# Tail-token loads split by head instead of by batch, and tail-token stores in one transfer, in a fused retention + SoLU kernel

## The chip, the cores and the metric

The kernel runs on one core of a Trainium2 chip. The metric is the device time of one execution in microseconds; the median of three runs is compared. A profile of one execution stands beside it. In the profile PE is the matmul engine (TensorE), PEld its weight loads, DVE the vector engine, ACT the scalar engine, POOL GpSimd, and SP the engine that issues nearly all transfers ("SPq" is its queue). The transfers themselves are carried out by 16 DMA engines.

## The reference

Eight batches, eight heads, 576 tokens per batch, head size 64. First a decayed causal attention without softmax, then a feed-forward layer with a SoLU and a layer norm on all 4608 tokens:

```python
scores = scale * q @ k.T                         # (8, 8, 576, 576)
ret    = scores * gamma_h ** (i - j) for j <= i  # else 0
x      = (ret @ v).transpose(0, 2, 1, 3).reshape(4608, 512)
h      = x @ w_in                                # (4608, 1024)
solu   = h * softmax(h)
ln     = (solu - mean) / sqrt(var + 1e-6) * g_ln
out    = ln @ w_out                              # (4608, 512), float32
```

## The kernel before

The 576 tokens of a batch are cut into two windows of 256 tokens and a rest of 64, the "tail". The tails of four batches together make one more window of 256 tokens, so that a group of four batches has nine windows and both groups have 18 (`WINS`; a window with index 2 is a tail). Each window is worked on in two halves of four heads: 36 steps `i`. The steps of the tails are 16 and 17 (batches 0 to 3) and 34 and 35 (batches 4 to 7). On the output side a window gives two tiles of 128 tokens: 36 tiles `t`, of which 16, 17, 34 and 35 hold tail tokens, two batches of 64 each.

For each step the kernel loads q, k and v (`load`: `ldq16` is the q of step 16) into buffers `rawq`, `rawk`, `rawv`, five of each, and scales or casts them to 16 bits (`sq`, `sk` at L394, `cv` at L399, in the main part of the kernel all on POOL). A full step is one transfer of 256 KB for each of q, k and v. A tail step is four transfers of 64 KB for each. TensorE transposes (L419, L429), forms scores (`S`, L508), the inter-window part and the product with v (L472); DVE applies the mask; ACT moves the result to `xT` (L576). For each tile TensorE then computes `M1` (L587), ACT the exponential (L595), DVE the SoLU and its statistics, TensorE transposes and computes `M2` (L660), and ACT scales and evicts it to `o_sb` (`oe`, L669). There are three buffers `o_sb`. `store` (`out16` is the store of tile 16) sends 128 rows of 2 KB to DRAM: whole tiles at L680, tail tiles at L685 in two transfers of 64 rows.

The order on every engine is fixed. `plan()` lists all operations with what they depend on and which buffers they hold, `FIRST` and `LAST` write out the order by hand for the start and the end, and in between each operation has a due time; `order_ops` turns that into the start order, and `emit` issues it. `parts` tells the planner how many transfers an operation has. SP issues in this order too: an issue that waits for a buffer or for a completion holds up all that stand behind it. Of the last tile only the second half of the eviction (`oz`) and the store are issued after a branch on a value that the kernel computes (`tc.If`); the other side of that branch, a slower general path, is not executed with these inputs.

The instructions that move the tail tokens in the built program have these shapes (outermost first, in elements): a tail load reads 32x4x128 from DRAM and writes 32x4x128; a tail store reads 64x512 and writes 64x512.

Of the kernel before, what the change touches and what calls it, by code (L numbers as in the profile page):

```python
# [308 lines left out]
def kernel(  # L309
# [10 lines left out]
    nc = tc.nc  # L320
    _, H, S, D = q.shape
# [46 lines left out]
    tk = [dict() for _ in range(NT)]  # L368
# [4 lines left out]
    def load(i, nm, src):  # L373
        w, hf = divmod(i, 2)
        b, wi = WINS[w]
        hh = slice(4 * hf, 4 * hf + 4)
        st[i]["r" + nm] = t = pools["raw"].tile([P, 4, 2, D], FP, tag=nm, name="raw" + nm)
        if wi < 2:
            nc.sync.dma_start(
                out=t, in_=src[b, hh, 256 * wi : 256 * wi + 256, :].rearrange("h (p j) d -> p h j d", j=2)  # L380
            )
        else:
            for r in range(4):
                nc.sync.dma_start(
                    out=t[32 * r : 32 * r + 32],
                    in_=src[b + r, hh, 512:S, :].rearrange("h (p j) d -> p h j d", j=2),
                )

    def scale(i, nm, base, eng):
# [283 lines left out]
    def store(t):  # L673
        w, c = divmod(t, 2)
        b, wi = WINS[w]
        if wi < 2:
            r0 = b * S + 256 * wi + P * c
            n = 64 if 22 <= t < 28 else P
            for r in range(0, P, n):
                nc.sync.dma_start(out=out[r0 + r : r0 + r + n, :], in_=tk[t]["osb"][r : r + n])  # L680
        else:
            for r in range(2):
                r0 = (b + 2 * c + r) * S + 512
                q_dma = nc.scalar if t == NT - 1 and r else nc.sync
                q_dma.dma_start(out=out[r0 : r0 + 64, :], in_=tk[t]["osb"][64 * r : 64 * r + 64])  # L685

    w_in_v = moe_w_in.rearrange("(c p) f -> p c f", p=P)
    w2_v = moe_w_out.rearrange("(c p) m -> p c m", p=P)
# [60 lines left out]
    def emit(o):  # L749
# [4 lines left out]
        tt = {"DVE": nc.vector, "POOL": nc.gpsimd}.get(eng)  # L754
        if k_ in ("ldq", "ldk", "ldv"):
            load(x, k_[2], dict(q=q, k=k, v=v)[k_[2]])
        elif k_ == "sq":
            scale(x, "q", 0, tt)
# [6 lines left out]
        elif k_ == "Le":  # L765
            tk[x]["lo"] = lo = 8 if wide(f"L{x}") else 8 * (x % 2)
            tk[x]["ev"] = tl_ev("first" if wide(f"L{x}") else "last", lo, lo + 8)
        elif k_ == "TL":
            st[x + 2]["ev"] = tk[x - 4]["ev"] = tl_ev(x, 0, 16)
            tk[x - 4]["lo"] = 8  # L770
        elif k_ in ("bnA", "bnB"):
            stats(x, k_ == "bnB")
        elif k_ == "lwi":
            w_load(x, w_in_v)
        elif k_ == "lwo":
            w_load(x, w2_v)
        elif k_ == "wg":
            w2_cast(x, eng)
        elif k_ == "gc":
            nc.vector.tensor_copy(out=gln, in_=cur["g"][:, 0:8])  # L780
        elif k_ == "cnt":
            count_a()
        elif k_ == "cs":
            count_b()
        elif k_ == "ci":
            nc.vector.tensor_copy(out=count, in_=cur["cs"][0:1, 0:1])
        elif name[:2] == "wi":
            w_in_cast(int(name[2]), name[3] == "b", copy)
        else:
            dict(  # L790
                T=qk_tp, L=ln_tp, K=kv_mm, I=inter, st=state, sc=state_cast, sm=state_next, S=scores, mask=mask, V=av, xe=x_ev, M1_=mm1,
                ex=exp_, so=solu, va=squares, fx=sums2, fin=final, rs=rstd, M2_=mm2, oe=o_ev, out=store, wc=w2_center,
                M=lambda _: mm2(NT - 1, 1), oz=lambda _: o_ev(NT - 1, 1), G=lambda _: g_tp(), WM=lambda _: w2_sum(), wm=lambda _: w2_mean(),
            )[k_](x)
# [4 lines left out]
    with tc.manual_schedule():  # L799
# [6 lines left out]
        for x in sbd[0]:  # L806
# [3 lines left out]
            out=ident, in_=ident, pattern=[[1, P]], compare_op=ALU.is_equal, fill=0.0, base=0, channel_multiplier=-1  # L810
        )
        tri = masks.rearrange("p m (j jq q) -> p m j jq q", j=2, jq=2)
        for n, first in ((P, P), (64, 0)):
            nc.gpsimd.affine_select(
                out=tri[:n, 0], in_=tri[:n, 0], pattern=[[-1, 2], [1, 2], [2, 64]], compare_op=ALU.is_ge,
# [100 lines left out]
    with tc.If(in_range < NT * P, preferred_fallthrough_block=False) as cmp:  # L916
        with tc.For_i(0, NT, 1) as t:
            general(t)
        for b in range(B):
            r0 = (b // 4 * 18 + b % 4 * 4) * P  # L920
            nc.sync.dma_start(out=out[b * S : b * S + 512, :], in_=rows[r0 : r0 + 512, :])
        for b in range(0, B, 4):
            r0 = (b // 4 * 18 + 16) * P
            nc.sync.dma_start(
                out=out[b * S : (b + 4) * S, :].rearrange("(b s) m -> b s m", s=S)[:, 512:S],
                in_=rows[r0 : r0 + 256, :].rearrange("(b s) m -> b s m", b=4),
            )
    with cmp.Else():
        o_ev(NT - 1, 1)
        store(NT - 1)  # L930
# [30 lines left out]
```

## Time and profile before

| | |
|---|---|
| Runs | 212.8, 212.13, 214.13 us; median 212.8 |
| Span of the profiled execution, first to last instruction | 210.9 us (the runs lie 1.2 to 3.2 us above it; its own whole time is not listed apart) |
| PE busy | 200.8 us, 95% of the span |
| DVE, ACT, POOL busy | 79%, 67%, 67% |
| Granted TensorE clock | 0.999 |
| Transfers | 64814 packets, 42.66 MB, 202 GB/s on average |

A row of the page's part on transfers gives the tile, the queue, the number of issues, the KB of each and the median time from issue to landing. A row of a timeline gives the start, the length, the engine, the line, the operation with its tiles and shapes, the number of instructions merged into the row, and in brackets the idle time before it and what ended it. For SPq the length is that of the issue, not of the transfer. A table of stages gives the busy time of each engine in a stretch of the span; its last two columns are the share of the 16 DMA engines' time that packets took and the GB/s moved.

### The profile page before, as it was taken

What the parts mean: (1) busy time and instruction counts of PE and PEld (TensorE: products, weight loads), DVE (VectorE), ACT (ScalarE), POOL (GpSimd) and SP (SyncE); (2) the same over time, 40 slices, a digit from 0 to 9 for tenths busy, and PEclk for the clock granted to TensorE, in tenths of its full rate; (3) what the DMA queues carried; (4) which work ended last, traced back from release to release, by engine and by line L of the source; (5) the groups of instructions that cost most, each with busy time, mean ns of one, the idle gap of its engine ahead of it and who ended that gap; (6) DMA issues with size and microseconds to landing.
All of it is one profiled execution on the core that took longest, in us unless ns stands there. A gap on an engine that the chain in (4) does not pass through costs nothing. (4 is left out here: it accounts for less than half of the span.)

```text
span 210.9 us, 10171 instructions
## 1 busy us (share of the span) xinstructions
PE 200.8 (95%) x4400; PEld 113.2 (54%) x4400; DVE 166.1 (79%) x279; ACT 141.7 (67%) x235; POOL 141.7 (67%) x240
## 2 busy tenths in 40 slices
PE   7986989999999999999999999999999999999992
PEld 2442654665566555555555555555666555554451
DVE  6565779997868898978898898889988998753760
ACT  2375787897666776776666777666767777573752
POOL 7434758999997975948787979797979792001110
PEclk9999999999999999999999999999999999999999
DMA  5999999999666559778999686776355222311224
GB/s 157 345 355 334 329 311 269 301 293 306 195 188 188 169 139 278 217 214 259 314 288 305 198 252 183 217 234 181 94 152 153 54 57 67 71 63 54 101 101 104
DMA packets 64814, 42.66 MB, mean 202 GB/s; under 512 B 3320, under 2 KB 58624, under 8 KB 64768
## 3 DMA queue, kind: packets, MB, share of 16 engines
q1 hardware_dynamic: 64528, 41.82, 68.4%
q8 instruction: 34, 0.56, 1.2%
q10 hardware_dynamic: 240, 0.18, 0.5%
q14 instruction: 12, 0.10, 0.2%
HBM read 32.55 MB, written 9.44 MB: 199 GB/s over the span
## 5 line engine op out<-in xcount | busy, mean ns | idle before, releaser
L587 PE MATMUL h_ps<-w_in,xT 128*128 128x512 f16 x288 | 68.5, 380 | 0.0
L660 PE MATMUL o_ps<-w2c,ev 128*128 128x512 f16 (+1 forms) x296 | 67.6, 373 | 0.0
L610 DVE TENSOR_TENSOR solu<-h_ps,e_sb 128x1024 f16<-128x1024 f32 x32 | 39.2, 1223 | 16.7 <-ACT e_sb L595 16.5
L595 ACT ACTIVATE e_sb<-h_ps 128x1024 f32<-128x1024 f32 x36 | 36.8, 1023 | 21.9 <-PE h_ps L587 20.4
L540 DVE TENSOR_TENSOR ret<-s_ps,masks 128x1024 f16<-128x1024 f32 x36 | 43.9, 1220 | 6.0 <-PE s_ps L508 5.4
L660 PEld LDWEIGHTS <-ev 128*128 128x128 f16 x296 | 28.7, 98 | 32.7
L616 DVE BATCH_NORM_STATS2 bs<-solu 128x6 f32<-128x512 f16 x64 | 43.6, 685 | 0.9
L587 PEld LDWEIGHTS <-xT 128*128 128x128 f16 x288 | 25.3, 98 | 29.1 <-ACT xT L576 0.8
L394 POOL TENSOR_TENSOR q<-rawq,small 128x512 f16<-128x512 f32 x34 | 35.4, 1042 | 7.3 <-DMA rawq<-in_q_dram 5.9
L669 ACT ACTIVATE o_sb<-o_ps,rs 128x512 f32<-128x512 f32 (+1 forms) x37 | 25.0, 676 | 21.8 <-PE o_ps L660 10.4
L394 POOL TENSOR_TENSOR k<-rawk,small 128x512 f16<-128x512 f32 x34 | 35.4, 1042 | 6.0 <-DMA rawk<-in_k_dram 5.9
L457 ACT COPY ev<-tl 128x1024 f32<-128x1024 f32 (+1 forms) x32 | 29.7, 932 | 4.7 <-PE tl L429 4.2
L576 ACT CAST xT<-xy 128x512 f16<-128x512 f32 x36 | 26.7, 742 | 3.0 <-PE xy L472 2.9
L571 POOL CAST sbd<-gg 64x256 f16<-64x256 f32 x64 | 25.4, 397 | 3.0
L562 POOL TENSOR_TENSOR gg<-gt,small 128x128 f32<-128x128 f32 x32 | 13.1, 409 | 16.9 <-DVE gt L557 16.5
L648 POOL TENSOR_TENSOR w<-mv,w 128x2 f32<-128x2 f32 x16 | 3.1, 194 | 27.8 <-ACT w L633 13.9
L399 POOL CAST v<-rawv 128x512 f16<-128x512 f32 x28 | 17.1, 609 | 0.2
L508 PE MATMUL s_ps<-ev 64*64 64x128 f16 x576 | 14.8, 218 | 0.3
L472 PE MATMUL xy<-ret,v 64*64 64x128 f16 x576 | 14.7, 217 | 0.0
L472 PEld LDWEIGHTS <-sbd 128*128 128x128 f16 x128 | 9.3, 98 | 9.3 <-issue 1.1
L446 PE MATMUL tl<-ident,solu 64*64 64x64 f16 x1024 | 14.2, 195 | 0.0
L846 PE MATMUL tl<-zeros 128*128 128x512 f16 x41 | 12.7, 445 | 1.3 <-DVE zeros L802 1.3
(71 smaller groups left out, 214.6 us busy)
## 6 DMA issues: line engine op xcount, KB each, us to landing
rawq<-in_q_dram SPq DMA_DIRECT2D x32, 256.0 KB, 5.1
rawk<-in_k_dram SPq DMA_DIRECT2D x32, 256.0 KB, 5.3
rawv<-in_v_dram SPq DMA_DIRECT2D x32, 256.0 KB, 5.1
out_dram<-o_sb SPq DMA_DIRECT2D x26, 256.0 KB, 3.1
out_dram<-o_sb SPq DMA_DIRECT2D x19, 128.0 KB, 2.3
wst<-in_moe_w_in_dram SPq DMA_DIRECT2D x4, 512.0 KB, 6.8
wst<-in_moe_w_out_dram SPq DMA_DIRECT2D x4, 512.0 KB, 7.1
rawq<-in_q_dram SPq DMA_DIRECT2D x16, 64.0 KB, 2.4
```

What stands on the lines that cost most here:

```text
L394: eng.tensor_tensor(out=t.rearrange("p j h d -> p h j d"), in0=st[i]["r" + nm], in1=g, op=ALU.mult)
L457: nc.scalar.copy(out=t[:, lo:hi].rearrange("p x (r w) -> p r x w", r=2), in_=tls[n].rearrange("p r x w -> p (r x w)").bitcast(FP).rearrang ...
L472: nc.tensor.matmul(start=(c, e) not in begun, stop=False, skip_group_check=True, **kw)
L540: nc.vector.tensor_tensor(out=d["ret"].rearrange("p e h j q -> p (e h) (j q)"), in0=d["s"].rearrange("p e h j q -> p (e h) (j q)"), in1=ma ...
L571: nc.gpsimd.tensor_copy(out=t[ee[e], :, :, ee[e]], in_=st[i]["gg"][ee[e]])
L576: nc.scalar.copy(out=xT[:, 2 * w : 2 * w + 2, 2 * hf : 2 * hf + 2].rearrange("p c h (q j) -> p c h j q", j=2), in_=xys[i][:, :, 0:256].rea ...
L587: nc.tensor.matmul(out=h_ps[:, hh], lhsT=xT[:, t, dc], rhs=w_in16[:, dc, hh], start=(dc == 0), stop=(dc == 3),)
L595: nc.scalar.activation(out=d["e"], in_=d["h"], func=ACT.Exp, accum_out=se[:, t : t + 1])
L610: nc.vector.tensor_tensor(out=d["solu"], in0=d["h"], in1=d["e"], op=ALU.mult)
L616: nc.vector.bn_stats(out=d["bs"][:, half], in_=d["solu"][:, half * 512 : half * 512 + 512])
L660: nc.tensor.matmul(out=o, lhsT=d["ev"][:, d["lo"] + c], rhs=w2c16[:, c, mm], start=(c == 0), stop=(c == 7))
L669: nc.scalar.activation(out=d["osb"][:, mm], in_=d["o", half], func=ACT.Copy, scale=ws[t // 2]["rs"][:, t % 2 : t % 2 + 1])
```

## The change

In `load`, a tail step still issues four transfers of 64 KB for each of q, k and v. Each was one batch with four heads on 32 partitions; each is now one head with four batches on 128 partitions. In `store`, a tail tile other than the last goes in one transfer of 128 rows and no longer in two of 64. The last tile keeps its two halves on two queues. The planner is not touched, so the order of all operations on all engines stays; SP issues three transfers fewer (tiles 16, 17 and 34).

```diff
         else:
-            for r in range(4):
+            for h in range(4):
                 nc.sync.dma_start(
-                    out=t[32 * r : 32 * r + 32],
-                    in_=src[b + r, hh, 512:S, :].rearrange("h (p j) d -> p h j d", j=2),
+                    out=t[:, h].rearrange("p j d -> p (j d)"),
+                    in_=src[b : b + 4, 4 * hf + h, 512:S, :].rearrange("r (p j) d -> r p (j d)", j=2),
                 )
...
         else:
-            for r in range(2):
-                r0 = (b + 2 * c + r) * S + 512
-                q_dma = nc.scalar if t == NT - 1 and r else nc.sync
-                q_dma.dma_start(out=out[r0 : r0 + 64, :], in_=tk[t]["osb"][64 * r : 64 * r + 64])
+            rows_t = out.rearrange("(b s) m -> b s m", s=S)[b + 2 * c : b + 2 * c + 2, 512:S]
+            if t < NT - 1:
+                nc.sync.dma_start(out=rows_t, in_=tk[t]["osb"])
+            else:
+                for r in range(2):
+                    (nc.scalar if r else nc.sync).dma_start(out=rows_t[r], in_=tk[t]["osb"][64 * r : 64 * r + 64])
```

In the built program a tail load now reads 4x32x128 from DRAM and writes 128x1x128 on the SBUF side; a tail store reads 128x512 and writes 2x64x512. The store stands at L684 in the changed file (L687 for the last tile).

## The prediction

> **What bounds the kernel now.** I read the page's part 1 first, then the table by stage, then the waits of SP's queue, then the transfers.
>
> ```profile
> PE 200.8 (95%) x4400; PEld 113.2 (54%) x4400; DVE 166.1 (79%) x279; ACT 141.7 (67%) x235; POOL 141.7 (67%) x240
> 20.00:48.00 28.00, 25.45 (x456) 15.63 (x459) 23.78 (x42) 23.23 (x42) 23.52 (x36) 1.00 1.12 303
> 160.00:205.00 45.00, 45.00 (x852) 23.96 (x851) 32.96 (x53) 28.91 (x50) 16.07 (x29) 1.00 0.28 80
> SPq L680 <- ACT o_sb L669: 53.8, 24, 5.3
> ```
>
> The second and third rows are stages: length, busy time of PE, PEld, DVE, ACT, POOL, granted clock, share of the 16 DMA engines, GB/s. TensorE is busy 95% of the span and 45.00 of 45.00 us late on: whatever stops it there is not won back. From 20 to 48 us the transfers are the limit (share above 1, 303 GB/s). SP waits 53.8 us for results to store, so its own issue time is covered in most places. TensorE needs the tail loads only through POOL; POOL's last wait for a transfer ends long before the first of them is used:
>
> ```profile
> 33.26 1.04 POOL L394 TENSOR_TENSOR k<-rawk,small 128x512 f16<-128x512 f32 x1 [0.22 <-DMA rawk<-in_k_dram]
> ```
>
> So a faster tail load earns nothing (POOL's waits from 36 us on name no transfer at all). The question is whether the new shapes make transfers slow enough to reach a buffer that ACT or POOL needs, or the end.
>
> **The change part by part.**
>
> *How many DMA engines carry a transfer.* Three windows of the DMA view each hold few transfers of one queue (packets, MB, share of 16 engines):
>
> ```profile
> q10 hardware_dynamic: 160, 0.04, 10.7%
> small<-small ACTq DMA_DIRECT2D x1, 39.0 KB, 2.4
> g_rows<-in_moe_g_ln_dram ACTq DMA_DIRECT2D x1, 4.0 KB
> ...
> q1 hardware_dynamic: 144, 0.26, 13.9%
> out_dram<-o_sb SPq DMA_DIRECT2D x1, 256.0 KB, 2.0
> ...
> q1 hardware_dynamic: 160, 0.26, 22.8%
> out_dram<-o_sb SPq DMA_DIRECT2D x2, 128.0 KB, 2.2
> ```
>
> The second (190 to 195 us) is one store of 128 rows: 144 packets, so 16 beside the data. The third (182 to 187) is two stores of 64 rows: 160 = 128 + 2x16. The first (0 to 4) is 128 rows of `small` and 8 rows of `g_rows`: 160 = 136 + 24, that is 16 + 8. One closing packet per engine in use explains all three: transfers with 128 or 64 outermost rows ran on 16 engines, the one with 8 on 8. The page's own sum agrees:
>
> ```profile
> q1 hardware_dynamic: 64528, 41.82, 68.4%
> rawq<-in_q_dram SPq DMA_DIRECT2D x16, 64.0 KB, 2.4
> rawk<-in_k_dram SPq DMA_DIRECT2D x16, 64.0 KB, 3.4
> ```
>
> Counting 512 packets for each of 96 whole loads, 128 for each of 48 tail loads (these are 64 KB, two of the three kinds shown), 128 and 256 for the two kinds of weights (4 each), 128 for 26 stores and 64 for 19, and 16 more for each of these 197 transfers, I get 64528. So the tail loads of 32 partitions also ran on 16 engines.
>
> The changed program's instructions carry, on the DRAM side, 4x32x128 for a tail load (outermost count 4: the batches) and 2x64x512 for a tail store (outermost 2), against 128 on the SBUF side; before, both sides began with 32 or 64. No transfer of this trace has different outermost counts on its two sides. Bounds: 16 engines as now (the SBUF side decides), or 4 and 2 (the smaller decides). The nearest row is `g_rows`, where an outermost count under 16 set the engines; I take 4 and 2.
>
> The Trainium skill, "DMA: Bandwidth & Descriptors", section "Why a DMA increments its semaphore by 16 and not by 1", says that the engine count is the largest number up to 16 that divides the slowest dimension on both sides. By that rule it is 4 and 2; the same page's advice under "Rules for kernel authors" to use one 128-partition transfer instead of two halves speaks for the change, and without the first rule the sum below would be zero.
>
> *Prices.* One store row of 2 KB: 13.9% of 16 engines in 5 us is 11.1 us over 128 rows, 87 ns. On two engines a store is 64 rows each, 5.6 us, against 0.7 us now. Fixed part: 2.0 us to landing less 0.7, so 1.3 us. Upper bound per row: the 64-row stores, 22.8% of 80 us over 128 rows, 142 ns. A whole 256 KB load at 303 GB/s takes 0.865 us, 16 KB on each engine; a 64 KB tail load on four engines also puts 16 KB on each, so it costs engines 0 to 3 as much as a whole load: 0.865 us, a tile 3.5 us.
>
> *Issues.* Loads stay 48 issues; stores lose three, of 0.55 us each (the L685 row below). The first two are covered by SP's waits for results; at the end the saved issue (from about 206.5, 0.55 long) lies before SP waits for the last half's result, which ACT ends at 206.75 + 0.47 = 207.22. Price 0; without the cover, -0.6.
>
> *The last stores.*
>
> ```profile
> 205.95 1.89 SPq L685 DMA_DIRECT2D out_dram<-o_sb  x3
> 206.75 0.47 ACT L669 ACTIVATE o_sb<-o_ps,rs 128x256 f32<-128x256 f32 x1 [0.41 <-PEq L916]
> 207.37 0.47 SPq L685 DMA_DIRECT2D out_dram<-o_sb  x1
> L685 SPq DMA_DIRECT2D out_dram<-o_sb x7: 466/551/757, 128.4 to 207.4; - x7
> DMA to landing us min/median/max: 2.3/2.5/2.9
> ```
>
> Tile 34's halves leave at 205.95 and about 206.5; the last half of tile 35 at 207.37 lands near 207.37 + 2.5 = 209.9, and the span ends 1.0 us later. After: tile 34 holds two engines for 5.6 us from 205.95, to 211.5; both halves of tile 35 leave four rows each on the same engines, 0.7 us; with 1.3 fixed, 213.5. That is +3.6 us (bounds: 0 on 16 engines; +7.1 at 142 ns).
>
> *The stores of tiles 16 and 17, then the loads of windows 34 and 35.* SP issues in a fixed order, and in the built program each transfer waits for the eighth before it.
>
> ```profile
> 128.39 1.19 SPq L685 DMA_DIRECT2D out_dram<-o_sb  x2
> 129.68 0.53 SPq L379 DMA_DIRECT2D rawq<-in_q_dram  x1
> ...
> 133.23 1.28 SPq L685 DMA_DIRECT2D out_dram<-o_sb  x2
> ...
> 138.28 0.36 SPq L680 DMA_DIRECT2D out_dram<-o_sb  x1
> ...
> 143.23 0.36 SPq L680 DMA_DIRECT2D out_dram<-o_sb  x1
> 143.68 2.48 SPq L384 DMA_DIRECT2D rawq<-in_q_dram  x4
> ...
> 151.42 1.15 SPq L680 DMA_DIRECT2D out_dram<-o_sb  x1
> ...
> 156.51 2.94 SPq L384 DMA_DIRECT2D rawv<-in_v_dram  x4
> 159.55 0.38 SPq L680 DMA_DIRECT2D out_dram<-o_sb  x1
> 162.29 0.69 ACT L669 ACTIVATE o_sb<-o_ps,rs 128x512 f32<-128x512 f32 x1 [0.61 <-PE o_ps L660]
> 167.23 0.69 ACT L669 ACTIVATE o_sb<-o_ps,rs 128x512 f32<-128x512 f32 x1 [0.66 <-POOL w L648]
> 168.06 0.41 PE L508 MATMUL s_ps<-ev 64*64 64x128 f16 x16
> ```
>
> Between two of these stores stand three whole loads (2.6 us per engine). On engine 0 from 128.4: store 5.6, loads 2.6, store 5.6, loads 2.6, store 0.7, loads 2.6, store 0.7: 20.4 us, so it is free at 148.8, where the tail loads already wait. Then 24 tail loads (20.8) and two stores (1.4) take it to 171.0. The store issued at 159.55 (tile 21) thus lands at 172.3. `o_sb` has three buffers, so the eviction of tile 24, at 167.23 now, waits 5.1 us. Behind it on ACT stand every later eviction and cast; on TensorE the next score product (168.06) needs the PSUM bank that this eviction reads until 167.92, so TensorE stops at once: 5.1 less 0.1, **+5.0 us**. The store at 151.42 (12 tail loads earlier) lands at 161.2, 1.1 us ahead of the eviction at 162.29. Bounds: 0 on 16 engines; at 142 ns two stores of 9.1 us add 7.0, so +12.
>
> *The first group, windows 16 and 17.*
>
> ```profile
> 53.27 2.62 SPq L384 DMA_DIRECT2D rawq<-in_q_dram  x4
> ...
> 75.89 1.83 SPq L384 DMA_DIRECT2D rawv<-in_v_dram  x4
> 86.08 0.61 POOL L399 CAST v<-rawv 128x512 f16<-128x512 f32 x1
> DMA to landing us min/median/max: 2.9/5.1/9.2
> ```
>
> From the first of these tiles to the last (four tiles between), engines 0 to 3 get six tiles 20.8 us, five whole loads 4.3, four stores 2.8: 27.9 from 53.3 is 81.2; with 2.9 - 0.9 = 2.0 for a load's landing (last row, L379) 83.2, while POOL casts it at 86.08. The cover is 2.9 us, price 0. If the engines stand idle in between, where SP waits for results, it goes: bound +4, as after that POOL's waits would be TensorE's.
>
> *Sum.* 0 + 3.6 + 5.0 + 0 = +8.6 us: the span goes from 210.9 to 219.5. The runs lie 1.2 to 3.2 above the span; on their median of 212.8 I forecast **221.4 us**.
>
> **The rivals.**
> *All transfers stay on 16 engines* (the SBUF side decides). For it: every 128-partition transfer here has 16. Against: `g_rows`. Then loads and landings stay, three issues go: 212.8, not slower. It decides where a 64 KB tail load still closes with 16 packets.
> *Only the end counts.* Engines 0 and 1 keep up: a row costs two engines alone less than 87 ns, or the backlog at 143.7 is worked off while SP waits. For it: only 1.1 and 5.1 us of lateness hang on sums of 20 us, and a tenth faster rows take most of it. Then +3.6: 216.4.
> *Two engines run at the 64-row price.* 142 ns a row: +7.1 and +12, 231.9. For it: that row, measured on 16 engines reading 64 partitions. Against: the new source is 128 partitions, as in the 87 ns row.
>
> **How the numbers follow.** Forecast, tail transfers on few engines with a stall at tile 24 and a late end: 0.62, own range 217.5 to 227 (the stall 1 to 6.5, the end 3.5 to 4, the first group 0 to 4). Only the end: 0.16. Sixteen engines: 0.12. The dear rows: 0.10. The range 215 to 228 leaves out the sixteen and the dear rows. About 1% (2.1 us) can be told from no change here: sixteen engines would be same, 0.10, or with luck at the end faster, 0.02; all else is slower, 0.88.
>
> **What would show it.** Queue q1 would hold 63862 packets: 64528 less 48x12 for loads closing with 4, less 3x30 for stores closing with 2; at 16 engines 64480. A store at L684 would land near 7 us, not 2.0 to 3.1. In the waits, ACT would wait once for a transfer of tile 21 near 167 us, and TensorE's busy share would drop there; the end would show SP idle some 3.6 us longer after its last issue. Wrong: tail loads landing in 2 to 3.5 us as now, or no gap on ACT near 167 us, or POOL waiting for `rawv` near 86 us, which would move the loss to the first group.

## The result and the profile after

The changed kernel takes 220.99 us (median of 6 runs, 220.62 to 222.46) against 212.77 us (6 runs): ratio 1.0394, 95% interval 1.0363 to 1.0426. Here and below the ratios compare runs in the chip's faster state alone and are not exactly the quotients of the medians given. The profiled execution has a span of 219.9 us, 9.0 us more than before.

From the page of the changed kernel, the busy times, the main queue (packets, MB, share of 16 engines) and the transfers:

```profile
PE 201.4 (92%) x4400; PEld 113.8 (52%) x4400; DVE 166.1 (76%) x279; ACT 141.5 (64%) x235; POOL 141.7 (64%) x240
q1 hardware_dynamic: 63862, 41.82, 64.5%
rawq<-in_q_dram SPq DMA_DIRECT2D x16, 64.0 KB
```

No engine has more instructions to work through than before: TensorE is busy 201.4 us against 200.8 for the same 4400 products and waits the rest. The packets are 63862, to the packet what loads closing on 4 engines and stores closing on 2 give. The rows of the transfers have no median time to landing at their end here, so the landings of the changed kernel are read from the waits and from the DMA view.

The two places of the loss stand in the waits of the engines and of SP's queue (total us, times, longest):

```profile
ACT o_sb L669 <- DMA out_dram<-o_sb: 2.7, 1, 2.7
PE s_ps L508 <- ACT o_sb L669: 1.7, 1, 1.7
SPq L918 <- SPq L918: 6.4, 1, 6.4
```

The first two are not in the profile before. The third stands there at L916, the same place in the file before:

```profile
SPq L916 <- SPq L916: 0.8, 2, 0.5
```

The first two, in order of time on ACT and TensorE of the changed kernel:

```profile
163.49 0.69 ACT L669 ACTIVATE o_sb<-o_ps,rs 128x512 f32<-128x512 f32 x1 [0.61 <-PE o_ps L660]
...
170.50 0.69 ACT L669 ACTIVATE o_sb<-o_ps,rs 128x512 f32<-128x512 f32 x1 [2.67 <-DMA out_dram<-o_sb]
...
171.24 0.42 PE L508 MATMUL s_ps<-ev 64*64 64x128 f16 x16 [1.73 <-ACT o_sb L669]
```

The eviction of tile 23 is 1.2 us later than before (162.29), that of tile 24 is 3.3 us later (167.23): some 2.0 us are lost between them, and TensorE stands still at the score product behind it. The rest is at the end (the issues of SP for tile 34 and for its half of tile 35):

```profile
209.14 0.64 SPq L684 DMA_DIRECT2D out_dram<-o_sb  x1
210.71 0.50 SPq L687 DMA_DIRECT2D out_dram<-o_sb  x1
```

SP's last issue is 3.3 us later than before (207.37), and from there to the end of the span it takes 9.2 us against 3.5: 5.7 us more. 1.2 + 2.0 + 5.7 is 8.9 of the 9.0 us.

How the four engines are kept busy shows in the DMA view of the changed kernel from 146 to 167 us, in 40 slices (busy tenths of 16 engines, then GB/s):

```profile
DMA  9999422222223222222268232224222222222422
GB/s 307 321 360 384 131 69 92 89 87 84 86 86 104 85 86 87 86 83 86 88 194 319 76 98 87 84 88 117 86 87 88 86 87 86 86 86 88 117 87 86
```

A level of 2 tenths and 86 GB/s: four of sixteen engines work without a break, the others rest except where a whole load, a store on 16 engines or another queue's packets pass. 64 KB at 86 GB/s is 0.76 us.

### The profile page after: what moved, and what is told of

Same layout as the page of the kernel before. It is cut to its first block, busy times and chain, and to the rows that moved or that the text cites. A ratio compares the mean times of both kernels' runs of the same rounds, so it can differ in the third digit from the quotient of the medians.

```text
span 219.9 us, 10167 instructions
## 1 busy us (share of the span) xinstructions
PE 201.4 (92%) x4400; PEld 113.8 (52%) x4400; DVE 166.1 (76%) x279; ACT 141.5 (64%) x235; POOL 141.7 (64%) x240
## 3 DMA queue, kind: packets, MB, share of 16 engines
q1 hardware_dynamic: 63862, 41.82, 64.5%
## 5 line engine op out<-in xcount | busy, mean ns | idle before, releaser
L540 DVE TENSOR_TENSOR ret<-s_ps,masks 128x1024 f16<-128x1024 f32 x36 | 43.9, 1220 | 10.1 <-PE s_ps L508 9.6
L446 PEld LDWEIGHTS <-solu 64*64 64x64 f16 x1024 | 10.9, 109 | 5.5 <-issue 2.9
```

Source lines behind the costliest of these rows:

```text
L446: nc.tensor.transpose(out=x[ee[e], r, c], in_=src[ee[r], P * c + 64 * e : P * c + 64 * e + 64], identity=ident[ee[r], ee[r]],)
L540: nc.vector.tensor_tensor(out=d["ret"].rearrange("p e h j q -> p (e h) (j q)"), in0=d["s"].rearrange("p e h j q -> p (e h) (j q)"), in1=ma ...
```

## The experiments

The runs are compared with the kernel before on the same chip; intervals are at 95%. The first four take the change apart.

**Loads only.**

The edit, against the kernel before; the stores stay as there:

```diff
-            for r in range(4):
+            for h in range(4):
                 nc.sync.dma_start(
-                    out=t[32 * r : 32 * r + 32],
-                    in_=src[b + r, hh, 512:S, :].rearrange("h (p j) d -> p h j d", j=2),
+                    out=t[:, h].rearrange("p j d -> p (j d)"),
+                    in_=src[b : b + 4, 4 * hf + h, 512:S, :].rearrange("r (p j) d -> r p (j d)", j=2),
                 )
```

> Tail loads by head, tail stores as before. Theory 'few engines': the loads run on four engines (queue q1 64528 - 576 = 63952 packets), a load costs these engines 0.76 us (86 GB/s over four engines in the late stretch of the changed kernel). Without the two slow stores of tiles 16 and 17 there is no backlog at 143.7 us, so 24 loads (18.2 us), two stores (1.4) and 1.3 fixed bring tile 21 to 164.6 us, before the eviction at 167.2: no stall, 212.8 to 214.0 us. Rival 'the loads alone make the stall': about 3.3 us slower than before, 216 us.

213.32 us against 213.46: ratio 1.0009 (0.9972 to 1.0047), 63952 packets. The loads do run on four engines, and alone they cost nothing that the times can show. ACT's eviction of tile 24 has its usual short wait for POOL:

```profile
167.54 0.69 ACT L669 ACTIVATE o_sb<-o_ps,rs 128x512 f32<-128x512 f32 x1 [0.66 <-POOL w L648]
```

**Stores only.**

The edit, against the changed kernel; the stores stay as there:

```diff
-            for h in range(4):
+            for r in range(4):
                 nc.sync.dma_start(
-                    out=t[:, h].rearrange("p j d -> p (j d)"),
-                    in_=src[b : b + 4, 4 * hf + h, 512:S, :].rearrange("r (p j) d -> r p (j d)", j=2),
+                    out=t[32 * r : 32 * r + 32],
+                    in_=src[b + r, hh, 512:S, :].rearrange("h (p j) d -> p h j d", j=2),
                 )
```

> Tail stores of tiles 16, 17 and 34 in one transfer, tail loads as before. Theory 'few engines': 64528 - 90 = 64438 packets; the stores of tiles 16 and 17 put some 5 us of backlog on two engines, which is hidden without the slow loads; the store of tile 34 costs 5.7 us at the end as in the changed kernel: 218.5 us, and no wait of ACT for a transfer. Rival 'the stall belongs to the stores': 221 us, with a wait of ACT near 167 us. Rival 'the end is a price of the loads too': under 217 us.

219.79 us, ratio 1.0303 (1.0213 to 1.0393), 64438 packets, no wait of an eviction on ACT for a store. The eviction of tile 24 has its short wait for POOL again:

```profile
168.52 0.69 ACT L669 ACTIVATE o_sb<-o_ps,rs 128x512 f32<-128x512 f32 x1 [0.66 <-POOL w L648]
```

The two slow stores in the middle are hidden: in this trace the evictions of tiles 16 to 19, behind which they run, take 14.8 us, as in the kernel before. The time is 1.3 us above the 218.5 expected, and as much above the next run, which has the last of the three stores alone. Of these 1.3 us, 0.8 stand in the two profiles ahead of the first tail transfer (the first eviction of an output tile starts at 47.9 us here and at 47.1 there), so they are not the price of a store.

**Only the store of tile 34.**

The edit, against the changed kernel (the queue is chosen so that tiles 16 and 17 stay on SP's):

```diff
-            if t < NT - 1:
+            if t == NT - 2:
...
-                    (nc.scalar if r else nc.sync).dma_start(out=rows_t[r], in_=tk[t]["osb"][64 * r : 64 * r + 64])
+                    (nc.scalar if r and t == NT - 1 else nc.sync).dma_start(out=rows_t[r], in_=tk[t]["osb"][64 * r : 64 * r + 64])
```

The loads go by batch, as in the kernel before.

> Only the store of tile 34 goes in one transfer; all else as before. Theory 'few engines': 64528 - 30 = 64498 packets, the same time as with all three stores, 218.5 us (+5.7), all of it behind SP's last issue. Rival 'the end is late because of what came earlier': 212.8 us.

218.48 us, ratio 1.0252 (1.0174 to 1.0331), 64498 packets. SP's queue of this kernel:

```profile
206.24 0.63 SPq L684 DMA_DIRECT2D out_dram<-o_sb  x1
207.53 0.51 SPq L687 DMA_DIRECT2D out_dram<-o_sb  x1
```

The waits of SP's queue in it:

```profile
SPq L918 <- SPq L918: 6.5, 1, 6.5
```

And the head of its page:

```profile
span 216.8 us, 10170 instructions
```

Up to the last issue it is level with the kernel before (207.53 against 207.37); then SP waits 6.5 us. Some 5 us of the loss (5.0 on the medians, 5.9 on the spans) belong to one instruction.

**The same shapes with tokens outermost.**

```diff
-  src[b : b + 4, 4 * hf + h, 512:S, :].rearrange("r (p j) d -> r p (j d)", j=2)
+  src[b : b + 4, 4 * hf + h, 512:S, :].rearrange("r (p j) d -> p r (j d)", j=2)
...
-  nc.sync.dma_start(out=rows_t, in_=tk[t]["osb"])
+  nc.sync.dma_start(out=rows_t.rearrange("r s m -> s r m"), in_=tk[t]["osb"])
```

> As the changed kernel (loads by head to 128 partitions, stores in one transfer of 128 rows), but the DRAM side names the same bytes with tokens outermost: 32x4x128 and 64x2x512 instead of 4x32x128 and 2x64x512. The tail tokens thus come to other partitions and other output rows than they should, so the tail part of the output is not the reference's; the work and the bytes are the same. Theory 'the outermost count sets the engines': 16 engines again, 64480 packets, 212.8 us within 0.7. Rival 'the shape is slow, not the count of engines' (128 partitions of 512 B, two blocks of DRAM in one store): 221 us as the changed kernel.

213.80 us against 213.46, ratio 1.0014 (0.9979 to 1.0050), and the queue's row of this kernel reads

```profile
q1 hardware_dynamic: 64480, 41.82, 66.8%
```

The same bytes, the same 128 partitions, the same number of issues, two blocks of DRAM in one store: all of the loss is gone with 16 closing packets back. It is the outermost count on the DRAM side, not the shape on the SBUF side. The order in which the bytes are walked changed with the count; that it is the count rests on the closing packets and on the 86 GB/s above. The run also shows what the change is worth without that fault: nothing. It is no replacement as it stands, since it puts the tail tokens on other partitions and other output rows; the rest of the kernel would have to follow.

The next four separate the two losses and test what stands between cause and time.

**Without the store of tile 34.**

```diff
-            if t < NT - 1:
+            if t < NT - 2:
...
-                    (nc.scalar if r else nc.sync).dma_start(out=rows_t[r], in_=tk[t]["osb"][64 * r : 64 * r + 64])
+                    (nc.scalar if r and t == NT - 1 else nc.sync).dma_start(out=rows_t[r], in_=tk[t]["osb"][64 * r : 64 * r + 64])
```

> The changed kernel, but tile 34 goes in two halves as before. Theory 'two separate losses': the end term of 5.7 us goes and the stall at tile 24 stays: 2.0 to 3.3 us over the kernel before, 215 to 216 us, with ACT waiting once for a transfer near 167 us. Rival 'all of it is the end': within 1 us of the kernel before.

215.72 us against 213.09, ratio 1.0096 (1.0061 to 1.0132). So about 1% is lost without the slow end, and the stall at tile 24 is there by itself:

```profile
169.82 0.69 ACT L669 ACTIVATE o_sb<-o_ps,rs 128x512 f32<-128x512 f32 x1 [2.11 <-DMA out_dram<-o_sb]
```

**Loads by head and the store of tile 34, tiles 16 and 17 in halves.**

```diff
-            if t < NT - 1:
+            if t == NT - 2:
...
-                    (nc.scalar if r else nc.sync).dma_start(out=rows_t[r], in_=tk[t]["osb"][64 * r : 64 * r + 64])
+                    (nc.scalar if r and t == NT - 1 else nc.sync).dma_start(out=rows_t[r], in_=tk[t]["osb"][64 * r : 64 * r + 64])
```

> The changed kernel, but tiles 16 and 17 go in two halves as before; loads by head and the one store of tile 34 stay. Theory 'the stall needs the backlog of both stores and the loads': no wait of ACT for a transfer, 5.7 us over the kernel before, 218.5 us. Rival 'the loads plus ordinary traffic suffice': the stall stays, 220.5 to 221 us.

218.68 us, ratio 1.0259 (1.0186 to 1.0332), no wait of an eviction on ACT for a store. So the stall needs both: the loads (absent in "stores only") and the two stores (absent here).

**Four buffers `o_sb`.**

```diff
-    e=2, solu=4, osb=3, tl=1, tlx=2, tlT=1, tlL=1, wst=5,
+    e=2, solu=4, osb=4, tl=1, tlx=2, tlT=1, tlL=1, wst=5,
```

> The changed kernel with four o_sb buffers instead of three; the order of all instructions is the same. Theory 'tile 24 waits for the buffer of tile 21': the eviction of tile 24 then needs tile 20, which lands earlier, so the stall of 2.0 us goes: 219 us. Rival 'the late transfers would stop something else instead' (POOL waiting for the loads of step 35): 221 us as the changed kernel.

219.77 us, ratio 1.0289 (1.0207 to 1.0371). No eviction waits for a store any more, and that of tile 24 has again the short wait for POOL:

```profile
169.06 0.69 ACT L669 ACTIVATE o_sb<-o_ps,rs 128x512 f32<-128x512 f32 x1 [0.66 <-POOL w L648]
```

The buffer was the link; no other wait took its place. The interval overlaps that of the changed kernel, so the trace carries this verdict, not the time.

**The store of tile 34 behind the branch.**

```diff
-            if o.name not in ("oz", f"out{NT - 1}"):
+            if o.name not in ("oz", f"out{NT - 2}", f"out{NT - 1}"):
                 emit(o)
...
     with cmp.Else():
         o_ev(NT - 1, 1)
+        store(NT - 2)
         store(NT - 1)
```

> The changed kernel, but the store of tile 34 is issued after the branch, right ahead of the last store. It leaves some 0.8 us later. Theory 'the wait for tile 34 stands ahead of SP's closing instructions, and 1.1 us of them that overlapped the last landing before now follow it': from landing to the end 0.9 us instead of 2.0, so the time is 0.3 us less than the changed kernel, 220.7. Rival 'the closing time belongs to the landing': 0.8 us more than the changed kernel, 221.8 us.

220.78 us, ratio 1.0334 (1.0254 to 1.0413): not to be told from the changed kernel by time. Against what was expected, the store leaves no later than it did, since SP waits for its data in either place (it is 0.4 us later, as everything is in this run from the eviction of tile 24 on, at 170.88 against 170.50). From its issue (209.51) to the end of the span (219.6) it takes 10.1 us, against 10.8 (209.14 to 219.9). SP's wait now stands with those of the program's end:

```profile
SPq L959 <- DMA out_dram<-o_sb: 5.8, 2, 5.6
```

In the four other runs with this one store on two engines and the wait ahead of the branch's end the same stretch takes 10.5 to 10.9 us. So some 0.4 to 0.8 us of the end term is the place of the wait: where it stands ahead of the end of the branch, SP's closing instructions start only when the store has landed. The expected 1.1 was too much.

## Why the prediction was right, and where its terms were off

**The engine count: right.** The step rested on `g_rows` and on the sum of packets, and the packet count of the changed kernel (63862) hit it exactly; so did those of the experiments, worked out the same way (63952, 64438, 64498, 64480). Of the two rules of the Trainium skill that were weighed (page "DMA: Bandwidth & Descriptors"), the one under "Why a DMA increments its semaphore by 16 and not by 1", the largest number up to 16 that divides the slowest dimensions of both sides, agrees with every packet count here. No run tells it from the plainer "the smaller count decides", since both give 4 and 2. The advice under "Rules for kernel authors", one 128-partition transfer instead of two halves, does not pay here: on 16 engines the time is that of the kernel before (ratio 1.0014), and on 2 engines the last of these stores costs some 5 us.

**The sum: close, in part by luck.** It was 8.6, against 9.0 on the spans and 8.2 on the medians. Of its terms the end was 2.1 too small, the stall 3.0 too large, and 1.2 us that the spans show ahead of the stall were not in it; these errors nearly cancel.

*The last stores* were put at +3.6 and are +5.7. Half of the error lies ahead of the landing: SP's 6.4 us of waiting from about 211.4 put it at 217.8, 8.6 us after the issue, where the prediction had 7.6 with tile 35's halves queued behind. The price of a row was right for the later rows. From 214.5 to 217.5 us the DMA view of the changed kernel has

```profile
q1 hardware_dynamic: 66, 0.13, 11.1%
```

11.1% of 16 engines in 3 us is 5.3 us over some 64 rows (0.13 MB), 83 ns a row against 87 assumed. The first rows went more slowly. The view from 209.5 to 220 us, in 40 slices of 0.26 us, shows

```profile
GB/s 0 0 0 31 31 8 55 16 23 31 47 31 62 109 164 203 226 265 133 62 55 55 47 55 55 47 47 55 55 31 31 0 0 0 0 0 31 0 0 0
```

From 210.3 to 212.4 us tile 34 alone moves some 30 GB/s, against some 50 at the end, after tile 35's halves have passed on all engines. At the later price these 64 KB would have taken 1.3 us and not 2.1: about 0.8 of the 1.0 us. Why the first rows are slow is open; in the run with only the store of tile 34 they are slow too.

The other half lies behind the landing: the prediction let the span end 1.0 us after it, as before, and it is 2.1. This wait stands ahead of the end of the branch; the last experiment moved it and got some 0.7 back. The rest is open.

*The stall at tile 24* was put at +5.0 and is +2.0. The store of tile 21 was worked out to land at 172.3; the eviction that waits for it starts at 170.50, so it landed at least 1.8 us earlier. The other 1.2 us are that the eviction itself is due later than before. The earlier landing comes from the price of a load: a tail load costs the four engines 0.76 us and not 0.865. The price was taken from 20 to 48 us, where all 16 engines share 303 GB/s, 18.9 each; four alone reach 86 GB/s, 21.5 each. Over 24 loads that is 2.5 us. Not all of it shows, as the stores of tiles 16 and 17 leave 0.7 and 1.1 us later than before. SP does not issue the store at 159.55 us either, as the prediction has it, but 6.4 us later, as each transfer waits in the program for the eighth before it and so for the slow loads:

```profile
165.98 3.19 SPq L680 DMA_DIRECT2D out_dram<-o_sb  x5
```

(The first of the five is tile 21.) The backlog thus stands partly in SP's queue and not in the engines', and the store's time from issue to landing alone would not show it. The landing is late either way, as the four engines are busy with these loads to 167 us and beyond. The mechanism is shown from three sides: the loads without the two stores do not stall, the stores without the loads do not, and a fourth buffer removes the wait.

*The first group* was put at 0 with a cover of 2.9 us. POOL waits for no `rawv` near 86 us (the cast starts at 86.00, before at 86.08). The profile of the changed kernel names a transfer for one wait of POOL near 66 us, 0.6 us long, ahead of a state product that reads no load; in the kernel before POOL waits 0.6 us at the same product, for DVE. TensorE lost nothing there: its busy time from 60 to 100 us is 40.00 of 40.00 in both kernels.

*The issues* were put at 0 and cost nothing, though the price was wrong (last section).

**What was not in the sum: 1.2 us before tile 24.** Two things make it up. By tile 20 the changed kernel is 0.7 us late (its eviction starts at 148.12, before at 147.45). Up to there it has one gap of TensorE without a named cause:

```profile
108.62 0.22 PE L446 MATMUL tl<-ident,solu 64*64 64x64 f16 x2 [1.09 <-issue]
```

Such gaps stand between 99 and 120 us in other kernels too: 0.31 us in the kernel before, 0.83 with the tokens outermost, 0.93 with four buffers. There is none with the loads only, and none without the store of tile 34, a kernel that up to its last stores is the changed one. They do not follow the change, so I count them as spread between executions, not as its effect. Their cause is open.

The other 0.5 us come between the evictions of tiles 20 and 23, and they do follow the change. This stretch takes 14.8 us in the kernel before and in the two with the stores changed alone, 15.0 to 15.2 with the loads by head but without the two slow stores or on 16 engines, and 15.3 to 15.4 in all four kernels with slow loads and both slow stores. TensorE counts as busy throughout, and no wait that the profile names stands behind it: this cause is open too.

**The rivals.** "All transfers stay on 16 engines" fell with the packet count. "Only the end counts" was half right on the sizes: the end is two thirds of the loss (5.7 of 9.0 us), but the stall is there alone in its own experiment. "Two engines run at the 64-row price" fell: the later rows on two engines took 83 ns, and even with the slow start the 72 rows of each engine (64 of tile 34, 8 of tile 35) took some 7.3 us, 0.10 us a row and not 0.142.

## What to carry to other kernels

Before a transfer is reshaped to fill more partitions, read the outermost count that its instruction carries on both sides: here 4 and 2 on the DRAM side cut the transfer to 4 and 2 of 16 engines, and naming the same bytes with a long dimension first gave all 16 back, at the price of another order of the tokens. Here slow transfers in the middle cost only what the cover of their buffers did not hold, and two causes that were free each cost 2.0 us together; the slow store near the end had no cover and was paid in full. Count packets: here the closing packets told the engine count in advance and bore it out after.

## What the runs showed of the hardware that was not expected

- In these runs the issue on SP's queue went with the shapes of the two sides, not with the number of engines. A tail load of 32x4x128 on both sides took 0.38 us at least; one to 128x1x128 took at least 0.53 on four engines and 0.54 on sixteen. From the view of line 384 (min/median/max ns), first of the kernel before:

```profile
L384 SPq DMA_DIRECT2D rawq<-in_q_dram x16: 378/430/1207, 53.3 to 154.1; - x16
```

the changed kernel:

```profile
L384 SPq DMA_DIRECT2D rawq<-in_q_dram x16: 528/564/1018, 52.9 to 158.7; - x16
```

and the kernel with tokens outermost:

```profile
L384 SPq DMA_DIRECT2D rawq<-in_q_dram x16: 541/602/2107, 53.7 to 157.3; - x16
```

- Four engines alone reached 21.5 GB/s each on rows of 512 B (86 GB/s in all), more than the 18.9 of each when all sixteen worked (303 GB/s, 20 to 48 us).
- Loads on a quarter of the engines cost nothing by themselves (ratio 1.0009); they cost 2.0 us where two slow stores queued ahead of them on these engines.
